# A projection load on ACT's queue, a zero-padded fifth chunk of v, and other prices in the planner of a fused attention and MLP kernel

## The chip, the cores and the metric

One core of one Trainium2 chip runs the whole program. The metric is the device time of one execution in microseconds (us). The engines are PE (matrix products; PEld is its weight load), DVE (vector), ACT (activations, copies), POOL (here reductions over partitions) and SP (which here only issues DMA transfers). Each engine runs its own list of instructions in order, and waits at semaphores for the others.

## The reference

Attention with a feature map over `w_phi`, for 8 batches of 8 heads with 576 tokens of 64 values, and behind it a two-layer MLP over all 4608 tokens:

```
proj = einsum('bhsd,df->bhsf', x, w_phi)                       # x is q or k; f = 128
proj = proj - max(abs(proj), axis=-1)
phi  = concatenate([exp(proj), exp(-proj)])
kv = einsum('bhsf,bhsd->bhfd', phi(k), v);  z = sum(phi(k), axis=2)
num = einsum('bhsf,bhfd->bhsd', phi(q), kv)
den = einsum('bhsf,bhf->bhs', phi(q), z) + 1e-06
x = num / den, heads side by side                              # 4608 x 512
h = x @ w_in                                                   # 512 x 2048, float64 weights
out = 0.5 * h * (1 + erf(h / sqrt(2))) @ w_out                 # 2048 x 512
```

## The kernel before

**Attention.** `k_quad(b, g)` takes four heads of batch `b`. It loads `kt` (k transposed, nine chunks of 128 tokens; the fifth chunk, `c == 4`, holds the last 64 tokens of two pairs of heads) and two tiles `vt` of v with a column of ones. Five units of one or two chunks follow: PE projects into `pk` with `wbd`, the block-diagonal `w_phi`; DVE takes the maximum (`mx`) and subtracts it (into `ek`, or in place in `pk`); ACT writes two exponentials `ek`; PE sums `ek` times `vt` in `kv`, by instructions that give 64 of the 128 rows of the result each. The fifth chunk uses 64 of the 128 rows of both operands (array shape 64*64), the others all of them (128*64). ACT copies `kv` to `kvn`. `q_pair(b, p)` does two heads in two halves: PE projects `qt` into `pq` (64*128), ACT copies that to `pc`, POOL reduces the maximum over partitions to `mb`, DVE subtracts it, ACT writes the exponentials `ef`, PE forms the numerators `pn` (128*64), and for the first two batches the denominators `pd` (128*32) too; for the others DVE and POOL form those (`un`, `db`). Numerators and inverse denominators pass through memory (`x_d`, `r_d`).

**Weights.** The float64 weights are turned into pairs of float32r tiles by `split_weights`: a load `raw_i` or `raw_o` of 1024 KB on SP, then seven steps: ACT's `Abs` into `wt` (L356), four DVE operations (L357, L359, L361, L363), ACT's cast into `w` (L334), DVE's subtraction into `w` (L340). `w_i0_q` and `w_i2_q` are the two tiles for the q-th quarter of the 2048 hidden columns, `w_o0` to `w_o14` those of the second product.

**MLP.** `block(j)` takes 256 tokens: DVE multiplies x by the inverse denominators and splits it into `xh` and `xl` (L340, L336), PE forms eight pairs of hidden columns in `ph` (24 products each; `ph_0_6` is the seventh pair of block 0, the first that uses the last quarter, `w_i0_3` and `w_i2_3`), ACT and DVE make `gh` and `gl` of them, PE sums those into `po` with `w_o`. The first eight blocks work so; the others in pairs by `wide_block` (`pa`, `pb`, `po`). All these products are full-array, 128*128.

**What sets the order.** Nothing runs in the order in which it is written. `Plan.order` is a planner that runs when the program is built: each `op(...)` names its engine, a price in us, what it reads and writes, and a rank; the planner keeps a clock per engine, gives each engine the startable operation of lowest rank, and adds prices for turns between array shapes (`SHAPE`, `BEHIND`, `BEFORE`), for ACT's tables and for loads (`kb`: kilobytes over one assumed rate in the order of issue). `emit` then writes all operations by planned start. A wrong price changes no result, only the place of an instruction in its engine's list. The constants at the end of the file (`T0`, `T15`, `LEAD`, `EARLY`, ...) set ranks and earliest times.

The start: DVE clears `idle`, ACT loads its table on it, PE runs `WARM` products `spin` over it; SP issues `w_st` (two loads into `wbd`), `kt`, `vt`, `qt`, `raw_i`, in this order.

Of the kernel before, what the change touches and what calls it, by code (L numbers as in the profile page):

```python
# [59 lines left out]
class Plan:  # L60
# [58 lines left out]
    def order(self, bias):  # L119
# [144 lines left out]
def mm_cost(m, n):  # L264
    return max(0.875 * m, n / 2.306 + 9) / 1e3
# [10 lines left out]
def act(n, psum=False):  # L276
    return (n / 1.2 + (51 if psum else 93)) / 1e3
# [15 lines left out]
def fused_kernel(ctx: ExitStack, tc: tile.TileContext, qT, kT, va, w_st, w_in, w_out, out):  # L293
# [116 lines left out]
    def k_quad(b, g, kvs, rank):  # L410
# [8 lines left out]
        op("sp", 0.06, lambda: nc.sync.dma_start(out=kt(), in_=kT[b, g]), w=kts, also=[kt], kb=590, **k())  # L419
# [24 lines left out]
        for u, (p, cs) in enumerate(units):  # L444
# [54 lines left out]
            for pp in (0, 1) if p is None else (p,):  # L499
# [4 lines left out]
                rs = slice(0, P) if p is not None else slice(64 * pp, 64 * pp + 64)  # L504
                last_u = (u == 2) if pp == 0 else (u == 4)
                for i, c in enumerate(cs):

                    def sums(acc=acc, rs=rs, c=c, i=i, es=es, first=fresh and i == 0, last=last_u and i == n - 1):
# [453 lines left out]
LEAD = 357.316
HOLD = 13.339
WR = -31.374
ATR = -1.296
T0 = 56.415
# [41 lines left out]
```

## Time and profile before

| | us |
|---|---|
| median of 3 runs | 1094.19 (1091.44 to 1094.27) |
| the profiled execution | 1094.28 |
| its span, first to last instruction | 1092.5 |
| PE busy in it | 1070.7 |
| DVE busy | 678.3 |
| ACT busy | 589.4 |
| POOL busy | 327.7 |

The span is what the profile sees of an execution; 1.8 us lie outside it. Busy time is a sum over stages that differ much: the attention of batches 0 and 1 and most of the weights come first, then MLP blocks mixed with the attention of the other batches, and from about 600 us MLP blocks alone. An operation's records in the profile can be more than its instructions: a float32 product (`kv`, `pn`, `pd`, `pq`, and `pk` of the first batches) gives two, a float32r product (`ph`, `po`, `pa`, `pb`) one. Matrix products overlap, so distances from start to start say more than lengths.

### The profile page before, as it was taken

How to read it: one execution, taken by the hardware profiler on the slowest of the kernel's cores; microseconds unless marked ns; L12 is line 12 of the kernel's file. 1: busy time of each engine (PE TensorE's matmuls, PEld its weight loads, DVE VectorE, ACT ScalarE, POOL GpSimd, SP SyncE). 2: the span in 40 equal slices, each digit the busy share in tenths (PEclk: the TensorE clock that was granted, in tenths of full speed). 3: DMA queues.
4: the chain of work that ended last, by engine and by line, in shares of the span. 5: the costliest groups of instructions: out<-in, count | busy, mean ns of one | idle time of the engine just before them, and what ended most of it. 6: DMA issues, size and time to landing. Idle time of an engine off the chain costs nothing.

```text
span 1092.5 us, 22042 instructions
## 1 busy us (share of the span) xinstructions
PE 1070.7 (98%) x8858; PEld 894.1 (82%) x8858; DVE 678.3 (62%) x1155; ACT 589.4 (54%) x1017; POOL 327.7 (30%) x116
## 2 busy tenths in 40 slices
PE   7899999999999999999999999999999999999998
PEld 4657868778778788788788999988989888898987
DVE  6999998688768657657659744335435436435332
ACT  6898788787778587777872212223223223223222
POOL 3243156676766665665651100000000000000000
PEclk9999999999999999999999999999999999999999
DMA  8787423323313313223116644426435434533421
GB/s 294 233 267 236 143 62 117 91 75 101 94 51 115 88 42 108 83 60 88 56 43 190 179 146 139 142 88 189 138 99 180 130 116 147 161 107 107 135 78 39
DMA packets 113735, 135.36 MB, mean 124 GB/s; under 512 B 26864, under 2 KB 80304, under 8 KB 111584
## 3 DMA queue, kind: packets, MB, share of 16 engines
q1 hardware_dynamic: 113632, 133.94, 40.4%
q8 instruction: 70, 1.15, 0.5%
q14 instruction: 33, 0.27, 0.1%
HBM read 106.30 MB, written 27.59 MB: 123 GB/s over the span
## 4 chain that ended last, share of the span: by engine, by line
PE 83%; DVE 8%; ACT 4%; issue 2%; DMA 1%; POOL 1%; SPq 0%; ACTq 0%; DVEq 0%; POOLq 0%
PE po L312 34%; PE ph L312 15%; PE pb L312 10%; PE pa L312 8%; PE kv L312 5%; PE pn L312 4%; PE pk L312 4%; PE pq L312 3%; ACT ek L497 1%; ACT ef L552 1%; POOL db L588 1%; DVE mx L489 1%; DVE ek L340 1%; DVE w_i L340 1%; DMA qt<-in_qT_dram 1%
## 5 line engine op out<-in xcount | busy, mean ns | idle before, releaser
L312 PE MATMUL po<-w_o,gh 128*128 128x512 f32 x1152 | 364.7, 398 | 0.0
L312 PEld LDWEIGHTS po<-w_o,gh 128*128 128x128 f32 x1152 | 204.7, 188 | 47.5 <-issue 11.5
L312 PE MATMUL po<-w_o,gl 128*128 128x512 f32 x576 | 227.5, 395 | 0.0
L588 POOL PARTITION_ALL_REDUCE db<-un x48 | 179.9, 3748 | 134.9 <-DVE un L585 94.0
L312 PE MATMUL ph<-xh,w_i 128*128 128x256 f32 x1024 | 197.0, 284 | 0.4 <-DVE gl L340 0.4
L546 POOL PARTITION_ALL_REDUCE mb<-pc x64 | 150.0, 2347 | 144.1 <-ACT pc L334 115.1
L312 PEld LDWEIGHTS ph<-xh,w_i 128*128 128x128 f32 x1024 | 162.7, 188 | 9.7 <-issue 7.4
L312 PE MATMUL ph<-xl,w_i 128*128 128x256 f32 x512 | 144.5, 282 | 0.0
L850 ACT ACTIVATE gh<-pa 128x512 fp32r<-128x512 f32 x40 | 24.0, 599 | 205.6 <-PE po L312 157.9
L312 PEld LDWEIGHTS po<-w_o,gl 128*128 128x128 f32 x576 | 108.3, 188 | 25.7
L312 PEld LDWEIGHTS kv<-vt,ek 128*64 128x64 f32 (+1 forms) x2560 | 84.6, 138 | 30.3 <-issue 11.1
L312 PE MATMUL pb<-b,s 128*128 128x256 f32 x720 | 98.5, 282 | 0.0
L312 PEld LDWEIGHTS ph<-xl,w_i 128*128 128x128 f32 x512 | 96.7, 189 | 1.7
L312 PE MATMUL kv<-vt,ek 128*64 128x65 f32 (+1 forms) x2560 | 94.1, 225 | 3.7 <-ACT ek L497 2.5
L497 ACT ACTIVATE ek<-ek 128x512 f32<-128x512 f32 (+1 forms) x140 | 81.7, 589 | 28.6 <-DVE ek L340 26.4
L312 PEld LDWEIGHTS pb<-b,s 128*128 128x128 f32 x720 | 91.5, 189 | 0.7
L552 ACT ACTIVATE ef<-pc 128x576 f32<-128x576 f32 x128 | 82.5, 682 | 9.4 <-DVE pc L340 8.4
L340 DVE TENSOR_TENSOR gl<-ph,gh 128x512 fp32r<-128x512 f32 x64 | 43.9, 686 | 60.3 <-ACT ph L679 60.0
L340 DVE TENSOR_TENSOR pc<-pc,mb 128x576 f32<-128x576 f32 x64 | 63.6, 994 | 24.3 <-POOL mb L546 24.1
L312 PE MATMUL pn<-ef,kvn 128*64 128x288 f32 x512 | 76.3, 420 | 2.2 <-ACT do L334 1.6
L489 DVE TENSOR_REDUCE mx<-pk 128x4 f32<-128x512 f32 (+2 forms) x90 | 51.3, 578 | 39.9 <-PE pk L312 39.0
L678 ACT ACTIVATE gh<-ph 128x512 fp32r<-128x512 f32 x64 | 38.3, 598 | 68.5 <-PE ph L312 66.7
(87 smaller groups left out, 1543.2 us busy)
## 6 DMA issues: line engine op xcount, KB each, us to landing
s<-s_d SPq DMA_DIRECT2D x160, 256.0 KB
kt<-in_kT_dram SPq DMA_DIRECT2D x16, 576.0 KB
qt<-in_qT_dram SPq DMA_DIRECT2D x64, 144.0 KB
x_d<-xo SPq DMA_DIRECT2D x64, 144.0 KB
out_dram<-ob SPq DMA_DIRECT2D x36, 256.0 KB
raw_i<-in_w_in_dram SPq DMA_DIRECT2D x8, 1024.0 KB
raw_o<-in_w_out_dram SPq DMA_DIRECT2D x8, 1024.0 KB
vt<-in_va_dram SPq DMA_DIRECT2D x16, 325.0 KB
```

What stands on the lines that cost most here:

```text
L312: return tc.keep_in_program_order(nc.tensor.matmul(*a, **kw))
L340: op(eng, cost, lambda: e.tensor_tensor(out=dst(), in0=a(), in1=b(), op=o), r=r, w=w, **kw)
L489: op("dve", dve(128 * n * nj, True), lambda view=view, mx=mx, js=js: nc.vector.tensor_reduce(out=mx()[:, 0].rearrange("p (j i) -> p j i", ...
L497: op("act", act(256 * n, inside), lambda at=at, es=es, s=s: nc.scalar.activation(es[s](), at(), AF.Exp, scale=1.0 - 2.0 * s), r=[parts[0][ ...
L546: op("pool", 2.2, lambda mb=mb, pc=pc: nc.gpsimd.partition_all_reduce(mb(), pc(), P, bass_isa.ReduceOp.absmax), r=[pc], w=[mb], **k(1))
L552: op("act", act(2 * HS), lambda ef=ef, pc=pc, s=s: nc.scalar.activation(ef()[:, s], pc(), AF.Exp, scale=1.0 - 2.0 * s), r=[pc], w=[ef], ta ...
L588: op("pool", 3.7, lambda db=db, un=un: nc.gpsimd.partition_all_reduce(db(), un(), P, bass_isa.ReduceOp.add), r=[un], w=[db], **k())
L678: op("act", act(2 * TB, True) + 0.016, lambda gh=gh, ph=ph: nc.scalar.activation(gh(), ph(), AF.Gelu), r=[ph], w=[gh], table="gelu", rank= ...
L850: op("act", act(2 * TB, psum) + 0.016, lambda gh=gh, at=at: nc.scalar.activation(gh(), at(), AF.Gelu), r=[at], w=[gh], table="gelu", rank= ...
```

## The change

The two loads of `w_st` go to ACT's queue (rank -900, and an operation of ACT depends there on the one before that writes the same buffer). The first `kt` is loaded in two parts. `WARM` is 2. Both `vt` tiles hold ten rows; in the fifth chunk the 64 rows that belong to the other pair of heads are zero, the ones column too, and its products use all 128 rows. The planner prices turns by `turn_cost`, and many prices and constants have other values.

```
-    BEHIND = {"f": 0.0, "k": 0.0, "q": 0.0, "v": 0.095, "n": 0.05, "d": 0.09, "s": 0.0}
-    BEFORE = {"f": 0.0, "k": 0.09, "q": 0.09, "v": 0.09, "n": 0.09, "d": 0.09, "s": 0.0}
-    SHAPE = {"f": 0, "k": 1, "q": 1, "v": 2, "n": 2, "d": 3, "s": 0}
+    TILED = {"k": 1, "q": 1, "v": 2, "n": 3, "d": 3}
+    ENTER, LEAVE, CROSS = 0.09, 0.105, 0.15
+
+    def turn_cost(self, a, b):
+        a, b = self.TILED.get(a, 0), self.TILED.get(b, 0)
+        return (self.ENTER if b and not a else 0.0) + (self.LEAVE if a and not b else 0.0) + (self.CROSS if {a, b} == {1, 2} else 0.0)
...
-                if self.SHAPE[last[0]] != self.SHAPE[o.kind]:
-                    cost += self.BEHIND[last[0]] + self.BEFORE[o.kind]
+                cost += self.turn_cost(last[0], o.kind)
...
-    return max(0.875 * m, n / 2.306 + 9) / 1e3
+    return max(0.875 * m, n / 2.226 + 2) / 1e3
...
-    return (n / 1.2 + (51 if psum else 93)) / 1e3
+    return (n / 1.2 + (96 if psum else 138)) / 1e3
...
-        op("sp", 0.06, lambda j=j: nc.sync.dma_start(out=diag(j), in_=w_st[64 * j : 64 * j + 64]), w=[wst], kb=33, rank=-400.0)
+        op("act", 0.6, lambda j=j: nc.scalar.dma_start(out=diag(j), in_=w_st[64 * j : 64 * j + 64]), w=[wst], kb=33, rank=-900.0)
...
-        op("sp", 0.06, lambda: nc.sync.dma_start(out=kt(), in_=kT[b, g]), w=kts, also=[kt], kb=590, **k())
+        first = [(slice(0, 2), slice(0, 4 * P)), (slice(2, 5), slice(4 * P, KC * P))]
+        at = k()
+        for us, cols in first if (b, g) == (0, 0) else [(slice(0, 5), slice(0, KC * P))]:
+            op("sp", 0.06, lambda cols=cols: nc.sync.dma_start(out=kt()[:, cols], in_=kT[b, g][:, cols]), w=kts[us], also=[kt],
+               kb=(cols.stop - cols.start) * 0.512, **at)
...
-            rows = slice(10 * p, 10 + 8 * p)
-            vt = sb["vt"]([P, 10 - 2 * p, D + 1], F32, f"vt_{nm}_{p}")
+            rows = slice(10 * p, 10 * p + 10)
+            vt = sb["vt"]([P, 10, D + 1], F32, f"vt_{nm}_{p}")
...
-                                        acc()[fs, 2 * s + j, :], lhsT=es[s]()[rs, j, i, fs], rhs=vts[c > 4]()[rs, 2 * c + j - 10 * (c > 4), :],
+                                        acc()[fs, 2 * s + j, :], lhsT=es[s]()[:, j, i, fs], rhs=vts[pp]()[:, at + j, :],
...
-WARM = 4
+WARM = 2
...
-HOLD2 = 2.448
+HOLD2 = 0
...
-PAIR_Q = 0.5
-PAIR_N = 1.18
+PAIR_Q = 0.686
+PAIR_N = 1.121
...
-PAIR_V = 0.125
+PAIR_V = 0.1175
...
-    va = np.ones((B, 2, P, 18, D + 1), v.dtype)
+    va = np.zeros((B, 2, P, 20, D + 1), v.dtype)
```

Other prices (POOL's reductions, DVE's small operations) and other constants (`T0` 56.415 to 65.576, `T15` 923.105 to 903.898, `LEAD`, `EARLY`, `WR`, `ATR`, `WPACE`, `WSPAN`, `PATIENCE`) change in the same way.

Three places of the order follow; `_0_0` in a name are batch and group, and the number at its end only tells tiles apart. First DVE's list from the start. Before:

```order
L336 CAST wbh_94<-wbd_68 128x256
L340 TENSOR_TENSOR wbl_96<-wbd_68,wbh_94 128x256
L489 TENSOR_REDUCE mx_0_0_0_116<-pk_0_0_0_0_101 128x2
L340 TENSOR_TENSOR ek_0_0_0_0_118<-pk_0_0_0_0_101,mx_0_0_0_116 128x256
L489 TENSOR_REDUCE mx_0_0_1_124<-pk_0_0_1_111 128x4
```

And with the change:

```order
L339 CAST wbh_102<-wbd_68 128x256
L343 TENSOR_TENSOR wbl_110<-wbd_68,wbh_102 128x256
L360 TENSOR_SCALAR wt_i0_0_100<-wt_i0_0_100 128x1024
L362 TENSOR_SCALAR wt_i0_0_100<-wt_i0_0_100 128x1024
L496 TENSOR_REDUCE mx_0_0_0_121<-pk_0_0_0_0_104 128x2
L364 SCALAR_TENSOR_TENSOR wt_i0_0_100<-raw_i0_0_88,wt_i0_0_100 128x1024
L343 TENSOR_TENSOR ek_0_0_0_0_130<-pk_0_0_0_0_104,mx_0_0_0_121 128x256
```

The first two steps on `wt_i0_0` now stand ahead of the first reduction of `pk`; before they stood behind the units 0 to 2. Second, ACT's list from the start, before:

```order
L317 ACT_TABLE_LOAD
L317 ACTIVATE idle_66<-idle_66 128x1
L334 COPY pc_0_0_0_126<-pq_0_0_0_0_120 128x288
L334 COPY pc_0_0_0_126<-pq_0_0_0_1_122 128x288
L497 ACTIVATE ek_0_0_1_140<-pk_0_0_1_111 128x512
```

And with the change:

```order
L331 DMA wbd_68<-in_w_st_dram 64x128
L320 ACT_TABLE_LOAD
L320 ACTIVATE idle_66<-idle_66 128x1
L331 DMA wbd_68<-in_w_st_dram 64x128
L359 ACTIVATE wt_i0_0_100<-raw_i0_0_88 128x1024
L359 ACTIVATE wt_i2_0_124<-raw_i2_0_98 128x1024
L337 COPY pc_0_0_0_134<-pq_0_0_0_0_126 128x288
```

The two `Abs` activations of the first weights moved from behind the first exponentials to ahead of ACT's first copy. Third, PE's list up to `ph_0_6`, before:

```order
L312 MATMUL kv_2_1_0_1920<-vt_2_1_0_1618,ek_2_1_1_0_1800 64x65 x2
L312 MATMUL kv_2_1_0_1920<-vt_2_1_0_1618,ek_2_1_1_1_1908 64x65 x2
L312 MATMUL pk_2_1_2_1980<-wbd_68,kt_2_1_1036 128x256
L312 MATMUL pk_2_1_3_1982<-wbd_68,kt_2_1_1036 128x256 x2
L312 MATMUL ph_0_6_1991<-xh_0_1251,w_i0_3_1784 128x256
```

And with the change:

```order
L315 MATMUL kv_2_1_0_1901<-vt_2_1_0_1510,ek_2_1_0_0_1772 64x65 x2
L315 MATMUL kv_2_1_0_1901<-vt_2_1_0_1510,ek_2_1_0_1_1803 64x65 x2
L315 MATMUL pk_2_1_2_1928<-wbd_68,kt_2_1_1072 128x256
L315 MATMUL ph_0_6_1932<-xh_0_1245,w_i0_3_1774 128x256
```

`ph_0_6` now comes ahead of the second unit's `kv` and of `pk_2_1_3`, and, further up, with fewer `pn` and `pq` in front of it.

## Rows read from the trace of the kernel before

**Rows 1.** From the head of the page: busy time of each engine with its share of the span, and its instructions.

```profile
PE 1070.7 (98%) x8858; PEld 894.1 (82%) x8858; DVE 678.3 (62%) x1155; ACT 589.4 (54%) x1017; POOL 327.7 (30%) x116
```

**Rows 2.** A table of stretches, in us from the start of the span: length; busy time (and records) of PE, PEld, DVE, ACT and POOL; the granted clock of PE; the busy share of the DMA engines and GB/s.

```profile
0.00:9.00 9.00, 6.73 (x20) 3.07 (x22) 1.53 (x5) 1.49 (x2) 0.19 (x4) 1.00 0.64 211
9.00:20.00 11.00, 8.08 (x144) 6.26 (x142) 8.90 (x16) 8.98 (x18) 4.77 (x2) 1.00 1.00 385
20.00:50.00 30.00, 25.18 (x406) 16.75 (x402) 29.37 (x50) 25.72 (x54) 11.23 (x5) 0.94 0.71 235
50.00:92.70 42.70, 38.26 (x532) 24.49 (x532) 40.59 (x60) 37.98 (x80) 18.83 (x8) 0.96 0.82 257
92.70:150.00 57.30, 56.88 (x510) 44.47 (x508) 54.31 (x66) 47.05 (x71) 14.46 (x6) 1.00 0.51 157
...
200.00:300.00 100.00, 100.00 (x945) 78.81 (x944) 80.78 (x119) 80.40 (x132) 71.75 (x25) 1.00 0.30 88
```

**Rows 3.** The longest waits of PE from 92.7 us to the end: who waited for whom, us in total, times, the longest.

```profile
PE pk L312 <- ACT pc L334: 1.6, 1, 1.6
PE pn L312 <- ACT xo L334: 0.5, 2, 0.3
PE ph L312 <- DVE gl L340: 0.4, 1, 0.4
```

**Rows 4.** The timeline around 150 us: start, length, engine, line, operation, tiles and shapes, records, and in brackets the idle time ahead of it with what ended it.

```profile
146.59 4.08 POOL L588 PARTITION_ALL_REDUCE db<-un  x1
...
147.14 3.54 DVE L340 TENSOR_TENSOR w_i<-wt_i,w_i 128x1024 fp32r<-128x1024 f32 x1
...
150.61 0.75 DVE L340 TENSOR_TENSOR pc<-pc,mb 128x576 f32<-128x576 f32 x1
...
151.76 0.68 ACT L334 COPY pc<-pq 128x288 f32<-128x288 f32 x2
...
152.19 1.56 PE L312 MATMUL pk<-wbd,kt 128*128 128x256 f32 x6 [1.60 <-ACT pc L334]
...
153.40 0.47 PE L312 MATMUL ph<-xh,w_i 128*128 128x256 f32 x1
```

**Rows 5.** The timeline of PE alone, in a stretch in which it doesn't wait.

```profile
232.78 1.19 PE L312 MATMUL pn<-ef,kvn 128*64 128x288 f32 x8
233.80 1.10 PE L312 MATMUL kv<-vt,ek 128*64 128x65 f32 x32
234.73 1.14 PE L312 MATMUL pn<-ef,kvn 128*64 128x288 f32 x8
235.80 0.68 PE L312 MATMUL kv<-vt,ek 64*64 64x65 f32 x16
236.42 0.39 PE L312 MATMUL pk<-wbh,kh 128*128 128x256 f32 x1
236.64 0.28 PE L312 MATMUL pk<-wbl,kh 128*128 128x256 f32 x1
236.76 0.27 PE L312 MATMUL pk<-wbh,kl 128*128 128x256 f32 x1
```

**Rows 6.** Groups of PE's records by shape: records, busy us and mean ns of one, idle time ahead.

```profile
L312 PE MATMUL kv<-vt,ek 128*64 128x65 f32 x2048 | 73.1, 225 | 2.6 <-ACT ek L497 1.7 <-ACT kvn L334 0.7
...
L312 PE MATMUL kv<-vt,ek 64*64 64x65 f32 x512 | 21.8, 224 | 1.0 <-ACT ek L497 0.8 <-ACT kvn L334 0.2
```

**Rows 7.** The timeline of the start (columns as in rows 4).

```profile
0.72 1.22 SPq L328 DMA_DIRECT2D wbd<-in_w_st_dram  x2
...
2.00 0.58 SPq L419 DMA_DIRECT2D kt<-in_kT_dram  x1
...
9.06 0.42 DVE L489 TENSOR_REDUCE mx<-pk 128x2 f32<-128x256 f32 x1 [4.83 <-PE pk L312]
...
10.18 0.76 PE L312 MATMUL pq<-qt,wbd 64*128 64x288 f32 x4 [0.70 <-DMA qt<-in_qT_dram]
...
10.96 0.70 ACT L334 COPY pc<-pq 128x288 f32<-128x288 f32 x2 [8.75 <-PE pq L312]
...
14.29 1.19 ACT L356 ACTIVATE wt_i<-raw_i 128x1024 f32<-128x1024 f32 x1
```

**Rows 8.** Transfers issued in the first 8 us: tiles, issuing queue, count, size of one.

```profile
raw_i<-in_w_in_dram SPq DMA_DIRECT2D x2, 1024.0 KB
kt<-in_kT_dram SPq DMA_DIRECT2D x2, 576.0 KB
qt<-in_qT_dram SPq DMA_DIRECT2D x4, 144.0 KB
vt<-in_va_dram SPq DMA_DIRECT2D x1, 325.0 KB
vt<-in_va_dram SPq DMA_DIRECT2D x1, 260.0 KB
```

**Rows 9.** Two steps of DVE's weight work, at places where POOL doesn't reduce.

```profile
76.30 0.68 DVE L357 TENSOR_SCALAR wt_o<-wt_o 128x1024 f32<-128x1024 f32 x1
...
87.11 1.22 DVE L340 TENSOR_TENSOR w_o<-wt_o,w_o 128x1024 fp32r<-128x1024 f32 x1
```

**Rows 10.** The timeline where block 0's input is ready and its first product starts.

```profile
90.18 1.21 DVE L340 TENSOR_TENSOR xl<-rb,xh 128x1024 fp32r<-128x1024 f32 x1
...
92.78 0.39 PE L312 MATMUL ph<-xh,w_i 128*128 128x256 f32 x1
```

More of the change, by code (lines that the diff above doesn't have):

```diff
@@ L430, in k_quad @@
         for p in range(2):
-            rows = slice(10 * p, 10 + 8 * p)
-            vt = sb["vt"]([P, 10 - 2 * p, D + 1], F32, f"vt_{nm}_{p}")
+            rows = slice(10 * p, 10 * p + 10)
+            vt = sb["vt"]([P, 10, D + 1], F32, f"vt_{nm}_{p}")
             vts.append(vt)
-            op("sp", 0.06, lambda vt=vt, rows=rows: nc.sync.dma_start(out=vt(), in_=va[b, g][:, rows]), w=[vt], kb=300, **k())
+            op("sp", 0.06, lambda vt=vt, rows=rows: nc.sync.dma_start(out=vt(), in_=va[b, g][:, rows]), w=[vt], kb=333, **k())
         kv = [None, None]
@@ L503, in k_quad, with sums @@
                 acc = kv[pp]
-                rs = slice(0, P) if p is not None else slice(64 * pp, 64 * pp + 64)
                 last_u = (u == 2) if pp == 0 else (u == 4)
                 for i, c in enumerate(cs):
-                    def sums(acc=acc, rs=rs, c=c, i=i, es=es, first=fresh and i == 0, last=last_u and i == n - 1):
+                    def sums(acc=acc, pp=pp, at=2 * c - 10 * pp if c != 4 else 8, i=i, es=es, first=fresh and i == 0, last=last_u and i == n - 1):
                         ins = []
@@ L513, in sums @@
                                     ins.append(mm(
-                                        acc()[fs, 2 * s + j, :], lhsT=es[s]()[rs, j, i, fs], rhs=vts[c > 4]()[rs, 2 * c + j - 10 * (c > 4), :],
+                                        acc()[fs, 2 * s + j, :], lhsT=es[s]()[:, j, i, fs], rhs=vts[pp]()[:, at + j, :],
                                         start=first and j == 0 and s == 0, stop=last and j == 1 and s == 1, skip_group_check=True))
                         return ins
-                    op("pe", 4 * PAIR_V, sums, r=[*e, vts[c > 4]] + ([] if fresh and i == 0 else [acc]), w=[acc], kind="v", **k())
+                    op("pe", 4 * PAIR_V, sums, r=[*e, vts[pp]] + ([] if fresh and i == 0 else [acc]), w=[acc], kind="v", **k())
                 if last_u:
@@ L918 @@
 SPK = 3
-THIRD_K = 0.36
+THIRD_K = 0.356
 OBT = "pc"
@@ L933 @@
 GATE = 60
-T15 = 923.105
+T15 = 903.898
 BIAS = 40
 STICK = 2
-PATIENCE = 0.564
+PATIENCE = 0.397
 URGE = -1000.0
-EARLY = -44.245
-WPACE = 3.914
-WSPAN = 63.659
-WARM = 4
+EARLY = -21.964
+WPACE = 3.847
+WSPAN = 73.653
+WARM = 2
 EARLY_PK = ("pp", "po")
@@ L950 @@
 EPACE = 20.0
-TF = 64.15
+TF = 66.419
 ND = 2
-LUMP = 1.843
+LUMP = 1.875
 LINGER = 4.379
 PAIR_K = 0.43
-FULL_K = 0.433
-PAIR_Q = 0.5
-PAIR_N = 1.18
+FULL_K = 0.432
+PAIR_Q = 0.686
+PAIR_N = 1.121
 PAIR_D = 0.55
-PAIR_V = 0.125
+PAIR_V = 0.1175
 PULL = -2000.0
[L962 to L966, printed above, removed]
+LEAD = 364.568
+HOLD = 11.297
+WR = -26.018
+ATR = 18.016
+T0 = 65.576
 VERBOSE = False
@@ L978, in _layout @@
     v6 = v.reshape(B, 2, 2, 2, S, D)
-    va = np.ones((B, 2, P, 18, D + 1), v.dtype)
+    va = np.zeros((B, 2, P, 20, D + 1), v.dtype)
     for p in range(2):
         full = v6[:, :, p, :, :512].reshape(B, 2, 2, 4, P, D).transpose(0, 1, 4, 3, 2, 5).reshape(B, 2, P, 8, D)
+        last = slice(64 * p, 64 * p + 64)
         va[:, :, :, 10 * p : 10 * p + 8, :D] = full
-        va[:, :, 64 * p : 64 * p + 64, 8:10, :D] = v6[:, :, p, :, 512:].transpose(0, 1, 3, 2, 4)
+        va[:, :, :, 10 * p : 10 * p + 8, D] = 1.0
+        va[:, :, last, 10 * p + 8 : 10 * p + 10, :D] = v6[:, :, p, :, 512:].transpose(0, 1, 3, 2, 4)
+        va[:, :, last, 10 * p + 8 : 10 * p + 10, D] = 1.0
     w_st = np.concatenate([w_phi, w_phi], axis=0)
```

8 lines of the change are left out of this document (4 added, 4 removed).

## The prediction

> **What bounds the kernel now.** I read the page first, then a table of stretches, the waits of PE, and the timeline at three places. The page makes it a PE kernel: PE is busy 98% of the span of 1092.5 us [rows 1]. The table of stretches says where that is not the whole truth. From 92.7 us on PE hardly stands still; but up to there DVE is the engine without a gap (29.37 of 30 us, then 40.59 of 42.7) and PE only follows it, and from 92.7 to 150 both are nearly full (54.31 and 56.88 of 57.3) [rows 2]. Behind 92.7 PE's three longest kinds of wait are 2.5 us together, 1.6 of it in one place [rows 3]. So the time is: when PE is released into work that no longer waits, plus the PE work then left, plus few waits, plus the end.
>
> The release has a definite place. `ph_0_6`, the first product of the seventh pair of hidden columns in block 0, is the first that needs the last weights of the first projection, `w_i0_3` and `w_i2_3`. DVE finishes `w_i2_3` at 150.68 (147.14 + 3.54). PE stands at a `pk` until 152.19, when ACT's copies of `pc` begun at 151.76 free its buffer, and starts `ph_0_6` at 153.40 [rows 4]. I call 153.40 the gate: ahead of it DVE decides, behind it PE.
>
> **The change part by part.**
>
> *PE work behind the gate.* A turn from one array shape to another can be priced by distances between starts [rows 5]. Eight records of `pn` take 1.02 with a turn only ahead of them (232.78 to 233.80) and 1.07 with one only behind (234.73 to 235.80); 16 records of `kv` 64*64 with a turn on both sides take 0.62 (to 236.42), where half of the unturned 32 `kv` (233.80 to 234.73) is 0.47. So a turn costs 0.10 ahead of itself and 0.05 behind, and behind a turn into the full array it is 0.10, since the first `pk` takes 0.22 and the next 0.12. That is 0.15 for a turn into a 64-column shape and 0.20 for one into the full array, which I take for `pq` too. In the two orders there are 275 turns before and 257 now: the 32 into 64*64 vanish, 14 others come. By these prices that is 2.2 us less PE work in the whole program, but only 0.7 of it lies behind the gate (193 turns there before, 186 now). Against it, PE now reaches `ph_0_6` with less done (the order rows of PE at the gate): 16 `kv` instructions (two records each, 0.058), 4 `pn` (0.24), 2 `pq` (like a `pn`, 0.24) and 2 `pk` (0.40; three take 1.21 from 152.19 [rows 4]) of the whole program have come to stand behind it: 0.9 + 1.0 + 0.5 + 0.8 = 3.2. Net PE work behind the gate: **+2.5 us**.
>
> *The padding.* The 256 products of the fifth chunk go from 64*64 to 128*64. The rows give both forms the same length, 224 and 225 ns [rows 6], and the same pace, 0.47 per 16 records [rows 5]. I take nothing. The Trainium skill (TensorEngine Tiling (Array Packing), When to Use Tiling) would have a contraction of 64 run as two row tiles, and its table gives up to twice the speed; by that, padding to 128 would give up 256 times 0.029, 7.4 us. The 64*64 rows show no such gain to lose, so the sum stays without it.
>
> *Start-up, the large term.* Before, DVE's first reduction starts at 9.06, on PE's first `pk` [rows 7]. The change brings that `pk` forward: half as many `spin`, `kt` issued first on SP at 0.72 instead of 2.00, the projection on ACT. But the order rows put other work ahead of the reduction. On DVE two steps on `wt_i0_0` stand before it, and on ACT the two `Abs` activations of `raw_i0_0` and `raw_i2_0` stand before the first copy of `pc`. Each waits for a megabyte that SP issues as its tenth and its twelfth load.
>
> When does that land? Up to the end of the first `raw_i` the loads were 1152 + 585 + 576 + 1024 KB [rows 8] and the two of the projection (64 x 128 float32, 32 KB each), 3.48 MB; 1.90 MB had moved by 9.0 (at 211 GB/s), and then 385 GB/s [rows 2] give 13.1. The first `qt`, 1.99 MB in, would by that have moved by 9.2; it released PE at 10.1 [rows 7], so a landing is 0.9 behind its bytes. Now the stream starts 1.28 earlier and has 0.07 MB more ahead (0.2): 13.1 - 1.3 + 0.2 + 0.9 = 12.9, an estimate. `Abs` takes 1.2 [rows 7], the two DVE steps about 0.7 each [rows 9], and the first reduction starts at 15.6 instead of 9.06. Of these 6.5 us, 1.4 is work that would have come later, so DVE loses 5.1. It idled 2.1 between 9 and 20 [rows 2] and can regain that at most: bound 3.0. The waits for PE among them cannot come again, as PE's products will be long done; waits for ACT can, since ACT's second `raw_i` comes 1.17 MB later, at 16.0, and its first copy at 17.2. Regaining nothing and waiting for one more step of ACT (1.2) makes the other bound, 6.3. I take **4.2 us later**, nearer the lower one, as DVE now has weight steps to do between the reductions. PE's first products fall into this wait.
>
> *DVE work ahead of the gate.* Compared row by row, DVE does the same up to `w_i2_3`, save three operations that now come later: the last step of block 1's split (`xl_1`, 1.21 [rows 10]), one subtraction in `pc` (0.75 [rows 4]), one step on `wt_o12` (0.68 [rows 9]): **-2.7**.
>
> *A collision.* That last operation took 3.54 where the same kind takes 1.22 [rows 9], beside a POOL reduction from 146.59 to 150.67 [rows 4]. Whether it meets one again the order doesn't tell: between -2.3 and 0, taken in the middle, **-1.2**.
>
> Gate now: 150.68 + 4.2 - 2.7 - 1.2, and 0.2 from DVE to PE: 151.2, against 153.40, -2.2. PE gets there earlier and waits. Its first `ph` came 1.4 behind `xl_0`, which ended at 91.39 [rows 10]; DVE does 3.3 less ahead of `xl_0` (a reduction and a subtraction of 512 columns, one step of 0.68, one of 1.22), so the first `ph` comes at about 93.7. From there to the gate PE had 60.6, 2.0 of it waits; now 5.0 less stands there (16 `kv`, 4 `pn`, 3 `pk`, 2 `pq`, 5 turns, and 4 `pd` at half a `pn`), so PE is there at 147.3 and waits some 4 us, every later product behind it. Sum: -2.2 + 2.5 = **+0.3**.
>
> The other edits (`HOLD2`, ranks, prices) act through the order alone. The waits behind the gate, 1.2 us by rows 3 once its 1.6 and 0.2 are taken off, I leave; bounds 0 and 3, as DVE has 20% free there [rows 2]. The sum is made against the profiled execution, 1094.28, 1.8 of which lie outside the span; the median of the runs shown is 1094.19. **Forecast 1094.6**, own range 1092.3 (delay 3.0, no collision) to 1097.9 (6.3, the same collision).
>
> **The rivals.**
>
> *The start-up costs DVE little.* For it: the holes of 2.1 us, 2.7 more in the 72.7 us up to 92.7 [rows 2], and that what DVE now does first it would have to do anyway. Against it: the landing of the first `raw_i` is a floor under the first reduction. At a delay of 0.8 and no collision the gate is 146.7 (PE is there at 144): 1090.1, and with the later waits gone 1088.9. It decides below a delay of 1.7.
>
> *ACT becomes the bound of the start: slower.* ACT's first copy moves from 10.96 to 17.2, 6.2 later, 2.4 of them work done ahead, and its exponentials then need DVE's subtractions, which start at 15.6: it is late by 4 to 5.5. It had 4.3 and 4.7 us free up to 92.7 [rows 2], which to me absorbs what it loses beyond DVE; but its exponentials hold DVE's buffers and PE's `kv`. If DVE's delay grows to 8 through that, the gate is 155.0: 1098.4, and 1100 with one more wait behind it. It decides from a delay of 7.2.
>
> *The padding costs*, by the halved pace named above: 1102. The rows of `kv` speak against it.
>
> *Better prices remove waits.* All that PE waits behind the gate is 1.2, so this alone gives 1093.4, inside my range.
>
> **How the numbers follow.** My case, with the last rival in it, 0.62; the fast start 0.20; ACT 0.15; the padding 0.03. A measurement of this kernel can tell about 0.3%, 3.3 us, from no change. Nearly all of my case lies within that, the fast start beyond it, and ACT and the padding beyond it on the other side: faster 0.20, same 0.61, slower 0.19. The range takes half of each outer case: 1089.6 to 1098.8.
>
> **What would show it.** DVE's first reduction at 15 to 16 us behind an ACT activation; PE idle for several us between 9 and 17; the first `ph` near 94; a PE wait of 3 to 5 us at `ph_0_6`, released by DVE's `w_i2_3`, near 151; all `kv` 128*64 at 225 ns. It is wrong if `w_i2_3` ends ahead of 148 or behind 154, if `kv` has a slower pace, or if more than 3 us of waits stand behind the gate.

## The result, and the profile after

The changed kernel takes 1099.72 us (median of six runs, 1097.51 to 1102.25) against 1094.17 before: ratio 1.0056 [1.0041, 1.0071], slower by about 5.6 us. The forecast was 1094.6 in a range of 1089.6 to 1098.8, so the prediction was wrong, and the time is that which it gave for the rival "ACT becomes the bound of the start" (1098.4 to 1100). The profiled execution took 1102.25, 1100.4 of it inside the span; it is the slowest of the six, and a second profiled execution (below, `changed_again`) has a span of 1096.4. Where a number of the first belongs to that execution alone, I say so.

The head of the page after, as [rows 1]:

```profile
PE 1067.6 (97%) x8854; PEld 893.8 (81%) x8854; DVE 684.2 (62%) x1155; ACT 593.7 (54%) x1019; POOL 330.3 (30%) x116
```

PE does 3.1 us less work and the span is 7.9 longer. The table of stretches of [rows 2], after:

```profile
0.00:9.00 9.00, 5.75 (x20) 2.96 (x20) 1.53 (x5) 1.49 (x2) 0.19 (x4) 1.00 0.76 246
9.00:20.00 11.00, 1.35 (x6) 0.90 (x8) 3.71 (x7) 2.88 (x4) 0.26 (x1) 0.63 0.89 338
20.00:50.00 30.00, 26.33 (x408) 18.52 (x405) 28.87 (x45) 25.09 (x53) 13.37 (x6) 0.91 0.63 200
50.00:92.70 42.70, 35.94 (x563) 23.75 (x558) 37.73 (x62) 35.68 (x76) 16.75 (x7) 0.96 0.80 248
92.70:150.00 57.30, 53.16 (x515) 41.52 (x512) 55.02 (x71) 47.96 (x75) 13.90 (x5) 1.00 0.55 174
```

Between 9 and 20 us DVE now works 3.71 us instead of 8.90, ACT 2.88 instead of 8.98, PE 1.35 instead of 8.08. From 50 to 92.7 DVE has 5.0 us free where it had 2.1. The chain that ended last says what the start waits for (start, length, what; "issue" is time in which the profile shows no wait):

```profile
1.63 6.04 DMA vt<-in_va_dram
...
7.69 7.40 DMA raw_i<-in_w_in_dram
...
15.11 1.13 ACT wt_i L359
...
16.26 0.70 DVE wt_i L360
...
16.99 0.04 DVE wt_i L362
...
17.60 0.42 DVE mx L496
```

And the timeline of the same stretch, as [rows 7]:

```profile
6.56 2.04 PE L315 MATMUL pk<-wbd,kt 64*128 64x128 f32 x16
6.58 0.29 DVE L339 CAST wbh<-wbd 128x256 fp32r<-128x256 f32 x1 [4.72 <-DMA wbd<-in_w_st_dram]
10.34 0.76 PE L315 MATMUL pq<-qt,wbd 64*128 64x288 f32 x4 [1.74 <-DMA qt<-in_qT_dram]
16.26 0.69 DVE L360 TENSOR_SCALAR wt_i<-wt_i 128x1024 f32<-128x1024 f32 x1 [8.92 <-ACT wt_i L359]
18.94 0.71 ACT L337 COPY pc<-pq 128x288 f32<-128x288 f32 x2
19.40 1.62 PE L315 MATMUL pq<-qt,wbd 64*128 64x288 f32 x4 [8.31 <-ACT pc L337]
20.52 0.63 PE L315 MATMUL pk<-wbd,kt 64*128 64x128 f32 x2
```

PE's first `pk` is done by 8.6. Then the first megabyte of weights comes at 15.09, ACT's `Abs` takes 1.12, DVE's two steps 1.4, and only then the reduction of that `pk` begins, at 17.60 instead of 9.06. ACT's first copy begins at 18.94 instead of 10.96, and until it has freed a buffer PE's second `pq`, and the `pk` queued behind it, stand for 8.31 us.

The load is issued late for a reason that is not its place in the byte stream: its issue on SP waits for `vt` (the chain, 1.63 + 6.04, then 7.69). The waits in SP's list say how that came about. Before, and then with the change:

```
L353 DMA raw_i_0_90<-in_w_in_dram 128x1024 [waits DMAHW2_49]
L356 DMA raw_i_0_88<-in_w_in_dram 128x1024 [waits DMAHW3_49]
```

The loads of this program share eight completion semaphores in turn, and a load is held until the eighth one before it has landed. The second part of `kt` is one load more. So the first `raw_i` waits now for the first `vt`, which was issued behind both parts of `kt`, and no longer for `kt` itself; its issue moved from 6.22 to 7.69 us although all that stands ahead of it on SP was issued earlier. The 7.69 belongs to this execution: in `changed_again` the issue came at 6.83, and `Abs` began at 13.92.

### The profile page after: what moved, and what is told of

Its sections match the earlier page's. It is cut to its first block, busy times and chain, and to the rows that moved or that the text cites. A ratio compares the mean times of both kernels' runs of the same rounds, so it can differ in the third digit from the quotient of the medians.

```text
span 1100.4 us, 22052 instructions
## 1 busy us (share of the span) xinstructions
PE 1067.6 (97%) x8854; PEld 893.8 (81%) x8854; DVE 684.2 (62%) x1155; ACT 593.7 (54%) x1019; POOL 330.3 (30%) x116
## 4 chain that ended last, share of the span: by engine, by line
PE 79%; DVE 12%; DMA 2%; ACT 2%; issue 2%; POOL 1%; SPq 0%; ACTq 0%; DVEq 0%; POOLq 0%
PE po L315 34%; PE ph L315 13%; PE pb L315 10%; PE pa L315 8%; PE kv L315 5%; PE pn L315 4%; PE pk L315 3%; PE pq L315 3%; DVE mx L496 2%; POOL db L594 1%; DVE pc L343 1%; DVE ek L343 1%; ACT ek L504 1%; DVE wt_i L364 1%; DMA raw_i<-in_w_in_dram 1%
## 5 line engine op out<-in xcount | busy, mean ns | idle before, releaser
L315 PE MATMUL ph<-xh,w_i 128*128 128x256 f32 x1024 | 200.5, 284 | 0.0
L552 POOL PARTITION_ALL_REDUCE mb<-pc x64 | 153.1, 2397 | 137.6 <-ACT pc L337 118.0
L315 PEld LDWEIGHTS kv<-vt,ek 128*64 128x64 f32 x2560 | 85.8, 140 | 29.9 <-issue 10.0
L315 PE MATMUL kv<-vt,ek 128*64 128x65 f32 x2560 | 92.7, 227 | 7.2 <-ACT ek L504 4.8
L588 DVE TENSOR_SCALAR un<-ef,kvn 128x288 f32<-128x288 f32 x96 | 52.9, 573 | 38.7 <-POOL db L594 30.8
L343 DVE TENSOR_TENSOR pc<-pc,mb 128x576 f32<-128x576 f32 x64 | 66.4, 1040 | 16.6 <-POOL mb L552 16.4
L315 PEld LDWEIGHTS pa<-b,w_i 128*128 128x128 f32 x480 | 67.4, 188 | 6.7
```

What stands on the lines that cost most here:

```text
L315: return tc.keep_in_program_order(nc.tensor.matmul(*a, **kw))
L343: op(eng, cost, lambda: e.tensor_tensor(out=dst(), in0=a(), in1=b(), op=o), r=r, w=w, **kw)
L552: op("pool", 2.35, lambda mb=mb, pc=pc: nc.gpsimd.partition_all_reduce(mb(), pc(), P, bass_isa.ReduceOp.absmax), r=[pc], w=[mb], **k(1))
L588: op("dve", dve(HS, fast=True) + 0.06, lambda un=un, ef=ef, one=one, j=j: nc.vector.tensor_scalar(out=un()[:, j], in0=ef()[:, 0, j], scala ...
```

## The experiments

Experiments that move operations keep everything else of the kernel, prices included, and put named operations at other places of the order that the planner made:

```
-        for o in sorted(self.done, key=lambda o: (o.start, o.n)):
+        todo = {o.n: o for o in sorted(self.done, key=lambda o: (o.start, o.n))}
+        seq = list(todo)
+        for a, b in MOVES:
+            seq.remove(a)
+            seq.insert(seq.index(b) + 1, a)
+        for o in (todo[n] for n in seq):
```

Each was compared with the kernel before on the same chip.

**The start's order put back, and put into the kernel before.** `changed_again` is the changed kernel once more. In `changed_start_back`, `MOVES` puts the seven steps on `wt_i0_0`, the `Abs` of `raw_i2_0` and that of `raw_o0` back to about the places they had before: the first `Abs` behind the copies of the second `pc`, the next behind the first `ef`, DVE's steps behind the reductions of units 0 to 2. `before_weights_first` is the reverse: in the kernel before, the two `Abs` stand ahead of ACT's first copy and DVE's two steps ahead of its first reduction.

> The changed kernel once more, beside the others on the same chip. All theories: 1098.5 to 1101, with DVE's first reduction at 16.5 to 18.5 us and `ph_0_6` 3 to 6 us later than before.

> The changed kernel with the steps on the first two weights back at the places that they had before (ACT's two Abs behind its first copies, DVE's steps on wt_i0_0 behind the first units); every other instruction stays where the change put it. Theory `start` (the loss is the wait for the first raw_i, which stands ahead of everything on ACT and DVE): DVE's first reduction at about 7.5 instead of 17.6, of which DVE keeps 6 to 9 us, and the gate comes 5 to 7 us earlier: 1092 to 1095. Theory `rest of the order` (the loss is in later waits and in DVE operations beside POOL reductions): 1097 to 1100. Theory `loads` (the loss is that raw_i lands later): 1096 to 1098, since raw_i lands as late as in the changed kernel.

> The kernel before with the two Abs moved ahead of ACT's first copy and two DVE steps on wt_i0_0 ahead of its first reduction; loads, warm-up, padding and all else as before. The first raw_i landed at 13.73 before, so the first reduction comes at 13.7 + 1.2 + 1.4 = 16.3 instead of 9.06; 1.4 of the 7.2 us is work done earlier. Theory `start`: DVE is 4 to 6 us later at the gate, 1098 to 1100. Theory `rest of the order`: DVE's later holes take it up, 1094 to 1096.

| | us | before | ratio |
|---|---|---|---|
| `changed_again` | 1099.28 | 1093.31 | 1.0063 [1.0051, 1.0075] |
| `changed_start_back` | 1094.99 | 1093.31 | 1.0014 [1.0006, 1.0023] |
| `before_weights_first` | 1098.42 | 1093.31 | 1.0051 [1.0038, 1.0064] |

Putting nine operations back takes 4.3 of the 6.0 us away; bringing four of them forward in the kernel before costs 5.1. The order of the start is most of the loss. One expectation failed: in the profiled execution of `changed_again`, the fastest of its six (1098.26), `ph_0_6` comes 1.0 us later than before, not 3 to 6. The timeline of `changed_start_back`:

```profile
7.47 0.42 DVE L501 TENSOR_REDUCE mx<-pk 128x2 f32<-128x256 f32 x1 [0.18 <-PE pk L320]
10.59 0.70 ACT L342 COPY pc<-pq 128x288 f32<-128x288 f32 x2 [7.79 <-PE pq L320]
...
57.98 0.82 DVE L365 TENSOR_SCALAR wt_i<-wt_i 128x1024 f32<-128x1024 f32 x1 [3.29 <-ACT wt_i L364]
```

The reduction starts 1.6 ahead of before, as the first `pk` came earlier, and the copy 0.4 ahead. That gain is not in the time: 1.7 us of loss are left, and there is a second hole at 58 us, where DVE waits for the `Abs` of the next weights.

**Which engine's place it is.** `changed_act_first` is `changed_start_back` with both `Abs` still ahead of ACT's first copy; DVE is free to reduce at once. `changed_one_abs_first` is the changed kernel with only the second `Abs` put behind the first `ef`.

> As `changed_start_back`, but the two Abs stay ahead of ACT's first copy of pc; only DVE's steps are back. DVE's first reduction comes at 7.5, but ACT's first copy and exponential at 17 to 19. If the loss of the start sits on ACT (its copies and exponentials hold PE's and DVE's buffers): 1098 to 1100, as the changed kernel. If it sits on DVE (its reductions behind the weight steps): 1095 to 1096, as `changed_start_back`.

> The changed kernel with only the second Abs (wt_i2_0) moved back to behind the exponentials ef_0_0_0; the first Abs and DVE's two steps stay ahead. ACT's first copy comes 2.8 us earlier (about 15 to 16), DVE's first reduction stays at 16.4 to 17.6. If the second landing on ACT counts: 1097 to 1098.5. If only the first landing counts: 1099 to 1100.

They took 1100.91 and 1099.75 against 1093.71: 1.0066 [1.0055, 1.0077] and 1.0061 [1.0046, 1.0076]. The timeline of `changed_act_first`:

```profile
6.97 0.42 DVE L501 TENSOR_REDUCE mx<-pk 128x2 f32<-128x256 f32 x1 [0.44 <-PE pk L320]
...
13.30 1.12 ACT L364 ACTIVATE wt_i<-raw_i 128x1024 f32<-128x1024 f32 x1 [10.51 <-DMA raw_i<-in_w_in_dram]
...
17.08 0.69 ACT L342 COPY pc<-pq 128x288 f32<-128x288 f32 x2
...
19.31 0.29 DVE L501 TENSOR_REDUCE mx<-pk 128x1 f32<-128x128 f32 x1 [9.60 <-PE pk L320]
```

DVE's first reduction is at 6.97, 2.1 ahead of before, and the loss is all there. DVE does what two units give it and then waits 9.60 us for a `pk` of the third, which stands on PE behind the `pq` that waits for ACT's copy. So ACT's place alone is enough. And of the two `Abs` the first is enough, with DVE's two steps behind it: in the profiled execution of `changed_one_abs_first` (the slowest of its six, 1104.17) the copy comes at 14.97, DVE's reduction at 17.52, and ACT then waits 5.30 for DVE.

```profile
20.97 0.60 ACT L509 ACTIVATE ek<-pk 128x512 f32<-128x512 f32 x1 [5.30 <-DVE pk L348]
```

Whether DVE's two steps would do it with ACT's list open these runs don't show, as the steps need that `Abs`.

**The loads, the warm-up and the padding.** In `changed_old_loads` the changed kernel's order stays; the projection is issued on SP first, `kt` is one load and there are four `spin`. The other three have the order of the kernel before: `before_padded` with the zero padding alone, `before_new_loads` with the loads and two `spin` of the change, `before_padded_new_loads` with both.

```
-        op("sp", 0.06, lambda j=j: nc.sync.dma_start(out=diag(j), in_=w_st[64 * j : 64 * j + 64]), w=[wst], kb=33, rank=-400.0)
+        op("sp", 0.06, lambda j=j: nc.scalar.dma_start(out=diag(j), in_=w_st[64 * j : 64 * j + 64]), w=[wst], kb=33, rank=-400.0)
...
+            for cols in (slice(0, 4 * P), slice(4 * P, KC * P)) if (b, g) == (0, 0) else (slice(0, KC * P),):
...
+                ins = nc.sync.dma_start(out=kt()[:, cols], in_=kT[b, g][:, cols])
```

> The changed kernel in its own order and with its padding, but with the projection on SP ahead of kt, kt in one load and four warm-up matmuls, as before. Theory `start`: raw_i0_0 is issued when kt lands (6.2) and not at 7.7, lands at about 13.7 and not 15.1, first reduction 16.3 and not 17.6: 1098 to 1099. Theory `loads`: 1094 to 1096. Theory `rest of the order`: within 1 us of the changed kernel.

> The kernel before with the zero-padded fifth chunk alone (both vt tiles of ten rows, its products 128*64, and those of the second pair now read vt_1); every instruction stays where it stood, so 30 of the 275 turns between array shapes vanish, 20 of the 193 behind the gate. Theory `padding free, turns cost 0.15 to 0.20 each`: PE's work behind the gate is 3 to 4 us less, 1089.5 to 1091.5 where the kernel before takes 1093.3. Rival `padding costs` (a padded product takes twice as long): 7.4 us more, about 1100. Rival `turns cost nothing here`: 1093 to 1094.

> The kernel before with the projection loaded on ACT's queue (its second half behind ACT's table load), the first kt in two parts and two warm-up matmuls; every other instruction stays where it stood. Theory `start`: DVE's first reduction at 7.5 instead of 9.06, of which DVE keeps 0 to 1.6 us: 1091.7 to 1093.3. Theory `loads`: raw_i0_0 now waits for the first vt instead of for kt and lands about 0.5 us later, and the waits for it cost what the earlier start gave: 1093 to 1095.

> The padding and the new loads and warm-up in the order of before (the projection's two loads both at the head of ACT's list). If the two act apart: the sum of both gains, 1088 to 1091.5. If the new loads take away what the padding gives, or the reverse: 1092 to 1094.

| | us | before | ratio |
|---|---|---|---|
| `changed_old_loads` | 1099.55 | 1093.31 | 1.0065 [1.0053, 1.0077] |
| `before_padded` | 1092.71 | 1092.83 | 1.0000 [0.9991, 1.0010] |
| `before_new_loads` | 1092.15 | 1092.83 | 0.9995 [0.9986, 1.0004] |
| `before_padded_new_loads` | 1092.51 | 1092.83 | 0.9998 [0.9989, 1.0008] |

None of these edits costs or gives anything that shows, in either order; the gain that one theory of each forecast for `before_padded` and for both edits together, 2 us and more, did not come. The load's later issue is not the loss either: with the old loads the order alone loses as much. The groups of `kv` by shape, of `before_padded`, stand beside [rows 6]:

```profile
L317 PE MATMUL kv<-vt,ek 128*64 128x65 f32 x2560 | 91.5, 224 | 4.0 <-ACT ek L502 2.8 <-ACT kvn L339 1.0
```

All 2560 records have one shape and 224 ns, as both shapes had.

**The second hole.** `changed_two_holes` is `changed_start_back` with the `Abs` that DVE waits for at 58 us six instructions earlier on ACT, ahead of two copies of `pc`.

> As `changed_start_back`, and ACT's Abs on wt_i0_1 moved six instructions ahead in ACT's list, from behind two copies of pc to behind the exponentials of the unit 1_0_1. There DVE waited 3.3 us for it near 57 us. Theory `second hole`: most of that wait goes, and the gate comes 1 to 2.5 us earlier: 1092.5 to 1094. Rival: the copies and exponentials that now come 1.2 us later on ACT cost DVE and PE as much: 1094.5 to 1095.5.

It took 1095.86 against 1092.83, 1.0026 [1.0015, 1.0036]: no gain. In the profiled execution the wait goes elsewhere:

```profile
56.55 0.69 DVE L365 TENSOR_SCALAR wt_i<-wt_i 128x1024 f32<-128x1024 f32 x1 [1.33 <-ACT wt_i L364]
...
60.74 0.69 DVE L501 TENSOR_REDUCE mx<-pk 128x4 f32<-128x512 f32 x1 [3.50 <-PE pk L320]
```

The 3.3 us became 1.3 on the `Abs` and 3.5 on a `pk`. PE comes to that `pk` without a wait behind its own products, which took longer here: its granted clock is 0.56 between 54 and 56 us and 0.59 between 56 and 58, where it is 1.00 in `changed_start_back`, and eight records of `pd` take 1.19 instead of 0.69. So this trace does not show what the hole is worth; the median shows that moving the `Abs` gains nothing.

**The wait of PE at the gate, taken away in the kernel before.** `before_abs_later` puts one `Abs` (of `wt_o14`) behind the copies of `pc` for which PE waits 1.60 in [rows 4]; `before_all_three` adds it to `before_padded_new_loads`.

> The kernel before with ACT's Abs on wt_o14 moved from ahead of the two copies of pc_2_1_1 to behind them. At the gate ACT stood 2.77 us at that Abs (it waits for DVE's w_i2_3, which frees its buffer), and PE stood 1.60 us at a pk for the copies behind it. By the reading of the gate (PE's 1.6 us there is ACT's order, DVE's w_i2_3 at 150.7 the floor) ph_0_6 comes 1.6 us earlier, at 151.8: 1091.7 where the kernel before takes 1093.3. If another wait takes its place: 1093 to 1094.

> `before_padded_new_loads` with the Abs on wt_o14 moved as in `before_abs_later`. If the 1.7 us less PE work behind the gate that the padded kernel's trace showed, the earlier start and the 1.6 us at the gate add up: 1089.5 to 1091.5. If they hide one another: 1092 to 1093.

1093.32 against 1093.71, 0.9996 [0.9984, 1.0007], and 1092.43, 0.9992 [0.9981, 1.0003]: no version here is clearly faster than the kernel before.

```profile
152.40 0.47 PE L317 MATMUL ph<-xh,w_i 128*128 128x256 f32 x1
...
159.97 0.72 PE L317 MATMUL pq<-qt,wbd 64*128 64x288 f32 x2 [0.53 <-DVE ek L345]
```

`ph_0_6` comes 1.0 us earlier than in [rows 4], half of that goes into a new wait of 0.53, and the rest is too small to show.

**POOL's part in DVE's time.** In three kernels POOL's reductions of batches 0 to 2 are replaced by clears of the same tiles, which leaves those maxima and denominators out:

```
-            op("pool", 2.2, lambda mb=mb, pc=pc: nc.gpsimd.partition_all_reduce(
+            op("pool", 2.2, lambda mb=mb, pc=pc: nc.gpsimd.memset(mb(), 0.0) if b < 3 else nc.gpsimd.partition_all_reduce(
```

> The kernel before without POOL's reductions of batches 0 to 2: a clear of mb (and of db, to one) stands in their place, so those denominators and shifts are left out; DVE's instructions are the same. Theory `collision` (DVE's operations run long beside POOL's reductions): w_i2_3 takes 1.2 instead of 3.5 us, the other long ones near it their usual length, and DVE's busy time up to the end of w_i2_3 falls from 135.4 to 125 to 128. Rival (they run long for another reason, such as DMA traffic): it stays above 132.

> The changed kernel without the same POOL reductions. Theory `collision`: DVE's busy time up to the end of w_i2_3 falls from 134.7 to 135.1 to 122 to 125, which is 2 to 3.5 less than `before_no_pool`: the work that was counted as moved behind the gate then shows. Rival: it stays above 131, and the difference between the two orders stays below 1.

> `changed_start_back` without the same POOL reductions. Theory `collision`: DVE's busy time up to the end of w_i2_3 falls from 136.4 to 122 to 125, as in `changed_no_pool`, and w_i2_3 ends 2 to 4 us before that of `before_no_pool`. Rival `holes of the order`: it ends no earlier, since idle time of DVE takes the place of the stretch.

One execution each: 1086.11 for the kernel before, 1088.37 for the changed one, 1086.50 with its start put back, beside 1093.43 for the kernel before with its reductions. Up to the end of `w_i2_3` the stretches are (columns as in [rows 2]), for the kernel before without the reductions

```profile
0.00:141.55 141.55, 129.35 (x1536) 92.05 (x1538) 125.37 (x195) 120.40 (x222) 12.84 (x24) 0.99 0.70 232
```

and for the changed kernel without them:

```profile
0.00:144.21 144.21, 126.66 (x1544) 90.93 (x1546) 122.28 (x193) 120.02 (x219) 12.55 (x24) 0.95 0.69 227
```

and with its start put back:

```profile
0.00:142.14 142.14, 129.18 (x1544) 93.21 (x1546) 122.52 (x192) 120.04 (x219) 12.09 (x24) 0.96 0.69 231
```

DVE's work there is 125.37, 122.28 and 122.52 us: without POOL's reductions the changed order has 3.1 or 2.9 less of it, about what the prediction counted (2.7). With them the three numbers are 135.38, 135.07 and 136.44 (next section). So the reductions lengthen DVE's work by 10.0 in the order of before and by 12.8 and 13.9 in the changed one.

But the gate gains nothing by the lesser work: `w_i2_3` ends at 144.21 and 142.14, behind the 141.55 of the kernel before, as DVE stands idle 21.9 and 19.6 us up to there against 16.2. Of the third expectation the first half came true, and of the second half the rival, `holes of the order`. Without the reductions the change costs 2.3 us where it costs 5.6 with them, and 0.4 with its start put back, where it costs 1.7; executions of one program differ by 3 us and more, so these two differences are rough.

## Why the prediction was wrong, step by step

The sum can be held against the traces term by term. DVE's time up to the end of `w_i2_3` is busy time plus idle time; then comes the way to `ph_0_6`, and the time behind it. The stretch up to the end of `w_i2_3` in the kernel before, in the first profiled execution after, in `changed_again` and in `changed_start_back`:

```profile
0.00:150.68 150.68, 135.72 (x1610) 95.48 (x1610) 135.38 (x195) 121.21 (x222) 50.15 (x24) 0.98 0.68 220
```

```profile
0.00:158.22 158.22, 130.75 (x1558) 93.03 (x1560) 135.07 (x192) 121.18 (x220) 50.80 (x23) 0.95 0.65 207
```

```profile
0.00:153.81 153.81, 130.72 (x1556) 93.41 (x1558) 134.74 (x192) 121.01 (x220) 49.23 (x23) 0.94 0.65 213
```

```profile
0.00:152.21 152.21, 132.56 (x1558) 94.27 (x1560) 136.44 (x192) 120.84 (x220) 50.80 (x23) 0.94 0.64 215
```

`ph_0_6` starts at 158.83, 154.43 and 152.80 in the last three. Against before (150.68, 135.38, `ph_0_6` at 153.40, span 1092.5) that gives, in us:

| | DVE idle | DVE busy | `w_i2_3` to `ph_0_6` | behind `ph_0_6` | span |
|---|---|---|---|---|---|
| predicted | +4.2 | -3.9 | -2.5 | +2.5 | +0.3 |
| after, first profile | +7.9 | -0.3 | -2.1 | +2.5 | +7.9 |
| `changed_again` | +3.8 | -0.6 | -2.1 | +2.9 | +3.9 |
| `changed_start_back` | +0.5 | +1.1 | -2.1 | +2.3 | +1.7 |

The first profile is the slowest execution of its six and that of `changed_again` the fastest of its six, so the medians (+5.6 and +6.0) lie between these two rows. DVE's idle time by stretches, in us:

| | 0 to 20 | 20 to 50 | 50 to 70 | 70 to 92.7 | 92.7 to the end of `w_i2_3` | sum |
|---|---|---|---|---|---|---|
| before | 9.6 | 0.6 | 0.5 | 1.6 | 3.0 | 15.3 |
| after, first profile | 14.8 | 1.1 | 4.8 | 0.2 | 2.3 | 23.2 |
| `changed_again` | 13.6 | 1.4 | 3.5 | 0.2 | 0.4 | 19.1 |
| `changed_start_back` | 9.1 | 0.8 | 3.6 | 0.2 | 2.1 | 15.8 |
| `before_no_pool` | 9.7 | 0.3 | 0.6 | 2.1 | 3.5 | 16.2 |
| `changed_no_pool` | 13.3 | 1.1 | 3.5 | 0.3 | 3.8 | 21.9 |
| `changed_start_back_no_pool` | 9.4 | 2.0 | 3.5 | 1.0 | 3.8 | 19.6 |

**The step that failed is DVE's work ahead of the gate, "-2.7" with the collision of "-1.2".** Of the -3.9 there came -0.3 and -0.6, and +1.1 where the start is put back. The count of operations was right: without POOL's reductions the changed order has 3.1 less work. What failed is the price. I took one collision that might go away, with bounds of -2.3 and 0; but DVE's operations are lengthened by POOL all along, by 10 us before, and with the change by 2.8 more in one execution of each. That is outside the bounds I gave, and it ate what the fewer operations saved. It is no accident of one trace: with the reductions, DVE's work up to the end of `w_i2_3` lies between 134.1 and 137.0 in the fourteen traces, seven of either order, and neither order has the lesser work. But POOL is not all that was missing. Without the reductions the work does fall, and idle time takes its place: 5.8 us more than in the kernel before, 3.4 with the start put back, 2.9 of either in the hole between 50 and 70 us. That hole is in every trace of the changed order in the table and stands nowhere in the sum. So fewer operations of DVE did not bring the gate forward in either case. The timeline at the gate after shows such lengthening (as [rows 4]):

```profile
151.51 3.75 POOL L594 PARTITION_ALL_REDUCE db<-un  x1 [27.70 <-DMA d_d<-do]
152.32 2.96 DVE L366 SCALAR_TENSOR_TENSOR wt_i<-raw_i,wt_i 128x1024 uint32<-128x1024 uint32 x1
155.17 2.67 POOL L552 PARTITION_ALL_REDUCE mb<-pc  x1
155.21 1.89 DVE L360 TENSOR_SCALAR wt_o<-wt_o 128x1024 f32<-128x1024 f32 x1
157.01 1.21 DVE L343 TENSOR_TENSOR w_i<-wt_i,w_i 128x1024 fp32r<-128x1024 f32 x1
```

`w_i2_3` itself kept its usual length, 1.21 instead of 3.54, though by the profile its first 0.8 us lie beside the end of the second reduction (155.17 + 2.67); spans on POOL are rough. The two operations ahead of it were lengthened, to 2.96 and 1.89 where their kind takes some 1.2 and 0.69, and `changed_again` and `changed_start_back` have the same two there (2.94 and 2.96, then 1.89). That makes 2.9 us above the usual lengths. In the last 12 us up to the end of `w_i2_3` before it is 4.9, as three steps ahead of it were lengthened too (2.16, 1.78 and 1.25, where their kinds take 1.22, 0.69 and 0.69). So at the gate itself the collisions did become less, by 2.0, within the bounds of the prediction; what ate the saving lies further ahead. The Trainium skill (SBUF — State Buffer, SBUF: two separate sides) says that DVE, in an operation with two inputs in SBUF, and a GpSimd operation that reads SBUF share a port pair under an exclusive lock, and that the loser blocks. The trace agrees that they meet (2.96 and 3.54 beside a reduction, 1.22 where POOL stands idle [rows 9]), but the step of 2.96 ends at 155.28, just behind the reduction's end at 155.26, so by these spans it did not wait for the whole of it before it began its own 1.2.

**The delay of the start** was about right in size, in part by luck, and wrong in parts. The start's order costs 4.3 us by the medians of `changed_again` and `changed_start_back`, against 4.2. In the second profile DVE's idle time grows by 3.8 in all, but that is 4.0 up to 20 us, 0.8 up to 50 and 3.0 in the hole behind it, less 4.0 of idle time behind 70 us that did not come again; the first profile has 5.2 up to 20 us and 7.9 in all. The landing was put at 12.9 from the bytes ahead of it; it was 15.09 in the first profile, and `Abs` started at 13.92 in the second. The stream did not start earlier for this load, because its issue hangs on an older landing. DVE's first reduction, forecast for 15.6, was at 17.60. The reason for the nearer bound, "the waits for PE among them cannot come again", held in the changed kernel, where DVE waits only 0.7 us for a `pk` up to the gate, but only because DVE's own two steps stand ahead of that wait: with them back, `changed_act_first` has DVE waiting 9.60 for a `pk`, through ACT's first copy.

**PE work behind the gate**, +2.5, was right: +2.5, +2.9 and +2.3. The waits behind the gate, which the prediction put at 1.2 (the lines of [rows 3] that stand there make 0.7), hardly moved: PE stands idle there 5.4 us before and 5.3, 5.6 and 5.5 after. The way to `ph_0_6` was about right too, -2.5 against -2.1. The picture of PE waiting 4 us there was not: PE started its first `ph` at 102.68 (100.66 in the second profile, 95.03 with the start put back), not 93.7. From there to `ph_0_6` it worked 53.4, 53.2 and 54.0 us, as the 53.6 that I counted, stood idle 2.7, 0.6 and 3.7, and did not stand at `ph_0_6` in any of the three. So PE came there as late as DVE. Of the signs that the prediction named, the first `ph` near 94 and the wait at `ph_0_6` did not come, and `w_i2_3` ended behind 154 in the first profile, though not in the second (153.81).

**The padding** costs nothing that shows: the interval of `before_padded` ends at 1.0010, 1.1 us. The Trainium skill (TensorEngine Tiling (Array Packing), When to Use Tiling) would have a contraction of 64 run in two row tiles; the 7.4 us that the prediction worked out from that are excluded as a price of the padding here. The rule itself is not tested: in the kernel before each group of eight such products uses one half of the rows, so the two row tiles never run by turns. The prediction's "same pace, 0.47 per 16 records" is not in [rows 5] for 64*64 (16 of them take 0.62 there, and the 0.15 above 0.47 were taken for turns); it is the run that shows it. In the one profile of `before_padded` the time behind `ph_0_6` is 1.7 shorter, which its 20 fewer turns there could give at 0.08 each, half my price; the medians don't show it, and this stays open.

**The rivals.** ACT as the bound of the start has the place and the time, and `changed_act_first` shows that its mechanism (ACT's copies, held by the two `Abs`, hold PE and so DVE) alone is enough; in the changed kernel DVE's two steps stand ahead of the same wait, and what either adds there is not told apart. I gave it 0.15, with a delay of 7.2 as the point from which it decides. The delay of the medians is 4.3, so it did not come by its own price but with the 3.9 us that DVE's work did not give back: that its time fits is luck. The fast start was ruled out by the landing.

**What stays open.** Of the 1.7 us that remain with the start put back, the work behind the gate is 2.3, which the way to `ph_0_6` all but takes back; what is left is DVE's lengthened work and the second hole, which I did not separate. `w_i2_3` ends 4.4 us apart in two executions of the changed program; 4.1 of that is idle time of DVE, 1.2 of it up to 20 us, and what sets it is not known. Without POOL's reductions `changed_start_back` is only 0.4 off, by one execution.

## What to carry to other kernels

Before a load-dependent operation is put ahead of others in an engine's list, ask what stands behind it and who frees a buffer with that: here one `Abs`, 1.1 us long, held a copy, the copy a product, and the product the engine that bounds. Count DVE's work with the prices of the stretch it runs in: where POOL reduces for a third of the time, fewer operations need not mean less time, and an order that saves work can lose as much in a hole elsewhere. And one more load can delay the issue of a large one behind it, when loads share semaphores in turn; here that delay cost nothing that shows.

## What was not expected of the hardware

The projection, issued on ACT's queue at 0.72 and, its second half, at 1.42 us, let DVE's `wbh` start at 6.58 us (5.54 to 7.29 in nine executions with this load); issued on SP ahead of `kt`, it let it start at 3.48:

```profile
3.48 0.29 DVE L336 CAST wbh<-wbd 128x256 fp32r<-128x256 f32 x1 [1.62 <-DMA wbd<-in_w_st_dram]
```

It seems that the small load fell in with the large ones issued in the same microseconds; no run separates that. The first `pk` still came earlier, with half as many `spin`: it begins at 8.31 before, where they run until 8.38, and at 6.56 after, where they run until 6.63, as it does in `changed_again`, where the projection was there by 5.54.

In the changed kernel PE's granted clock is 0.63 between 9 and 20 us, after PE has stood idle; one `pq` of four records takes 0.76 ahead of that and 1.62 behind it, so it ran at the lower of its two levels. `changed_start_back` has a clock of 0.69 there too and does not lose the 4.3 us, so the clock is not what the start costs.
